# Retention followed by a gated feed-forward layer: the second layer's 512-column products issued as two 256-column products

## The chip, the cores and the metric

The kernel runs on one core of one Trainium2 chip. The metric is device time in microseconds (us), as the median of several runs; lower is better. The profile is one further execution, taken by the hardware profiler.

## What is computed

The first half is a retention layer: for every batch and head a 64 x 64 state decays by a factor gamma and takes up the outer product of k and v at every token; the output is q times the state. The second half is a feed-forward layer with a short convolution as its gate. Cut to what matters:

```python
# B, H, S, D = 4, 8, 768, 64; d_model 512, d_ff 1024
state = gamma * state + k[t] outer v[t]
y[t] = scale * q[t] @ state
x = y as (B, S, 512)
h = relu(x @ w_in)                       # first layer, 512 -> 1024
gate = sigmoid(conv3(h, conv_w))         # over neighbouring tokens
out = (h * gate) @ w_out                 # second layer, 1024 -> 512
```

## The kernel before

The tokens are worked through in 24 steps of 64 tokens of two batches; three steps make a unit of 384 rows, and there are 8 units. TensorE (PE) does three kinds of work: the retention's small products (64 x 64, `multiply`, line 592), the first layer (`mm1`, line 743: 12 products for each of 8 blocks of hidden channels and each unit, with 382 to 386 moving columns) and the second layer (`mm2`, lines 818 to 825). To keep accuracy, each operand is split into a head and a rest in fp32r, and a product of two such operands is three products: head by head, head by rest, rest by head.

`mm2(u, t, p, h)` takes tile t (128 rows) of unit u and the pair p of hidden blocks: two blocks of 128 channels, three products each. The stationary operand is 128 x 128 values of g (gated hidden values); the moving operand is w[:, cs], a slice of the second layer's weights. `columns` (line 814) gives the slice: all 512 columns, except for the very last tile, which is done as two halves of 256 columns (h = 0, 1). The sum over the 4 pairs is gathered in one PSUM bank (2 KB a partition, 512 fp32 columns) of the four called ps_yo; `put` (line 833, ScalarE) then copies it to SBUF, and a DMA writes it out. The first layer's sums lie in two banks called ps_m, which `relu` (line 760, ScalarE) empties.

Every matmul in fp32 or fp32r brings its own weight load: in the trace each MATMUL has its LDWEIGHTS, which the profile lists as a row of its own engine name, PEld.

The order of each engine's work is written out by hand, letter by letter, in the table `ORDER` (lines 65 to 88); `o` in PE's string is one call of `mm2`. The function `plan` (line 273) goes through these strings with a cost for each task, and sets only in which order the engines' tasks are recorded against each other and which buffer each one takes. `list_tasks` (line 141) holds the costs; line 262 is that of `mm2`.

Of the kernel before, what the change touches and what calls it, by code (L numbers as in the profile page):

```python
# [20 lines left out]
DM, DFF = H * D, 1024  # L21
# [3 lines left out]
NF = DFF // P  # L25
# [107 lines left out]
def act(n, fixed=85):  # L133
    return fixed + n / 1.2, 110 + fixed + n / 1.2


def matmul(n):
    return max(113, 4.7 + 0.4427 * n)


def list_tasks():
# [3 lines left out]
    def task(key, engine, ns, after=(), take=(), free=(), count=0):  # L145
        after = [a if isinstance(a[0], tuple) else (a, 0) for a in after or () if a]
        tasks[key] = (engine, *ns, after, list(take), list(free), count)

    def load(key, n_bytes, after=(), take=()):
        task(key, DMA, (DMA_ISSUE, n_bytes), after, take)  # L150

    def pe(key, ns, after=(), take=(), free=(), count=0):
        task(key, PE, (ns, ns + 165), after, take, free, count)
# [10 lines left out]
    for n in range(N_STEPS):  # L164
        c, u = n % NC, UNIT_OF[n]
        first, width = FIRST_STEP[u], UNITS[u]
# [7 lines left out]
        if wide:  # L174
            pe(("scores", n), 1250, [("load_q", n), ("load_k", n)], banks, count=16)
            for j in range(2):
                last = [("g", "t")] if (n, j) == (WIDE - 1, 1) else []
# [29 lines left out]
    for i in [*range(NF), CONV, *range(NF, CONV)]:  # L207
        n = NF * 3 if i == CONV else 512
# [10 lines left out]
    for u, width in enumerate(UNITS):  # L219
        n0, n1 = FIRST_STEP[u], FIRST_STEP[u] + width  # L220
        body, cols = G * width * C, G * (TOKENS[u][1] - TOKENS[u][0])
        x = [("x_rest", n) for n in range(n0, n1 + (TOKENS[u][1] % C > 0))]
        for f in range(NF):
            p, odd = divmod(f, 2)
            h, cv, g = ("hc", ("h", u, p)), ("hc", ("cv", u, p)), ("g", (u, p))
            before = [("w_rest", f), f and ("mm1", u, f - 1)]
            take = [("ps_m", (u, f))]
            n = cols
            if u == 0 and f < SPLIT:
                n = G * P  # L230
                after = [("w_rest", f), f and ("mm1_wide", f - 1), ("x_rest", 0), ("x_rest", 1)]
                pe(("mm1_wide", f), 12 * matmul(n), after, take, count=12)
                before, take, n = before + [("mm1_wide", f)], [], cols - n
# [20 lines left out]
    for u, width in enumerate(UNITS):  # L254
        for p in range(NP):
            tiles = sorted(range(width), key=lambda t: u == LAST[0] and t != 1)
            for t, h in [(t, h) for t in tiles for h in range(1 + ((u, t) == LAST))]:
                cols = DM // (1 + ((u, t) == LAST))
                o, ps, g = ("t2", ("o", u, t, h)), ("ps_yo", ("o", u, t, h)), ("g", (u, p))
                need = [("g_rest", u, p), p and ("mm2", u, t, p - 1, h), ("w_rest", NF + 2 * p), ("w_rest", NF + 2 * p + 1)]  # L260
                ends = t == width - 1 and cols * (h + 1) == DM
                pe(("mm2", u, t, p, h), 6 * matmul(cols), need, [] if p else [ps], [g] * ends, 6)
                if p == NP - 1:
                    task(("put", u, t, h), ACT, act(cols, 45), [("mm2", u, t, p, h)], [o], [ps])
                    if u == LAST[0]:
                        load(("out", u, t, h), 4 * P * cols, [("put", u, t, h)])
                    else:
                        pieces = 1 + (t * P // (width * C) < ((t + 1) * P - 1) // (width * C))
                        task(("out", u, t, h), POOL, (550 * pieces, 550 * pieces + 1850), [("put", u, t, h)])
# [84 lines left out]
def retention_then_gated_ffn(  # L354
# [12 lines left out]
    nc = tc.nc  # L367
# [36 lines left out]
    ps_st = psum.tile([P, G, NPAIR, D], F32, name="ps_st")  # L404

    tasks = list_tasks()
    emitted, slot, more = plan(tasks)

    tiles = {}

    def buf(name, owner):

        if (name, owner) not in tiles:
            label = f"{name}_{slot[name, owner]}"
            if name in sizes:
                made = pool.tile([P, sizes[name]], F32R if name in ("xu", "g") else F32, name=label, bufs=1)
            else:
                made = psum.tile([P, 512], F32, name=label, bufs=1)
            tiles[name, owner] = made
        return tiles[name, owner]  # L420
# [23 lines left out]
    def g_of(u, p):  # L444
        t = UNITS[u] * C
        return buf("g", (u, p))[:, : 4 * G * t].rearrange("p (i f b t) -> p i f b t", i=2, f=2, b=G)
# [270 lines left out]
    def w_parts(i):  # L717
        return [split[i][:, k] for k in range(2)]
# [95 lines left out]
    def columns(u, t, h):  # L814
        return slice(h * DM // 2, (h + 1) * DM // 2) if (u, t) == LAST else slice(0, DM)

    @emits
    def mm2(u, t, p, h):
        cs = columns(u, t, h)
        ps = buf("ps_yo", ("o", u, t, h))[:, : cs.stop - cs.start]  # L820
        for f in (2 * p, 2 * p + 1):
            hi, lo = (g_of(u, p)[:, i, f % 2].rearrange("p b t -> p (b t)")[:, t * P : (t + 1) * P] for i in range(2))
            w_hi, w_lo = w_parts(NF + f)
            for i, (g, w) in enumerate(((hi, w_hi), (hi, w_lo), (lo, w_hi))):
                nc.tensor.matmul(ps, g, w[:, cs], start=(f == 0 and i == 0), stop=(f == NF - 1 and i == 2))  # L825

    def put_tiles(u, t, h):
        cs = columns(u, t, h)
# [23 lines left out]
    for i in range(WARM_SMALL):  # L852
        j, cross, at = i % 2, i // 2 % 2, i // 4 * D
        ps = banks[cross + 2 * (at // 512)]
# [81 lines left out]
```

## Time and profile before

| what | value |
|---|---|
| median of 3 runs | 340.3 us |
| lowest and highest run | 340.2 and 342.24 us |
| profiled execution, span from first to last instruction | 537.5 us |
| mean granted TensorE clock in the profiled execution | 0.560 |
| PE busy | 533.2 us, 99% of the span |
| weight loads (PEld) busy | 380.3 us, 71% |
| VectorE (DVE) busy, ScalarE (ACT) busy | 206.4 us, 188.6 us |

The profiled execution is 1.58 times as long as the median run: the power throttle granted the array 0.56 of its clock throughout it after the first 6.7 us. No separate device time is listed for the profiled execution; its span is what the views divide up. PE's busy time is the union of its matmuls from start to modelled end; since matmuls are pipelined, the mean duration of one matmul is longer than its distance to the next.

### The profile page before, as it was taken

Reading aid. Unit: us, or ns where it says so; the run is one execution under the profiler, and the core shown is the slowest. Engines: PE = TensorE matmul, PEld = TensorE weight load, DVE = VectorE, ACT = ScalarE, POOL = GpSimd, SP = SyncE. Lnnn points to the kernel's source line nnn. Section 1 sums busy time; section 2 is a strip of 40 time slices with the busy share of each in tenths; the row PEclk is TensorE's granted clock in tenths of the full one; section 3 lists DMA queues with packets and bytes.
Section 4 is the critical chain, followed back from the end, with each engine's and each line's share of the span. In section 5 each row is a group of like instructions: output and inputs, shape, how many; then the busy total and the mean of one; then the engine's idle time right before and its main releaser. Section 6 shows DMA issues by size and latency. Waiting matters only on the chain.

```text
span 537.5 us, 9902 instructions
## 1 busy us (share of the span) xinstructions
PE 533.2 (99%) x4315; PEld 380.3 (71%) x4315; DVE 206.4 (38%) x323; ACT 188.6 (35%) x367; POOL 36.9 (7%) x96
## 2 busy tenths in 40 slices
PE   9999999999999999999999999999999999999997
PEld 6988887777667577767767676776676676666575
DVE  2644247747555332603345021524133213333300
ACT  3757356353425423302425120442134023422301
POOL 1000000110002000010002000100001000200100
PEclk7555555555555555555555555555555555555555
DMA  8763693401225032113024000100001000100101
GB/s 291 233 238 129 191 330 97 141 4 38 79 71 205 0 79 79 61 39 99 21 79 146 32 1 0 40 21 1 0 1 40 20 1 20 34 6 1 48 11 59
DMA packets 20935, 40.15 MB, mean 75 GB/s; under 512 B 2854, under 2 KB 3116, under 8 KB 20892
## 3 DMA queue, kind: packets, MB, share of 16 engines
q1 hardware_dynamic: 19100, 34.01, 19.2%
q0 software_dynamic: 1792, 5.51, 3.3%
q8 instruction: 34, 0.56, 0.4%
q14 instruction: 9, 0.07, 0.0%
HBM read 33.21 MB, written 6.29 MB: 73 GB/s over the span
## 4 chain that ended last, share of the span: by engine, by line
PE 99%; ACT 0%; issue 0%; DVE 0%
PE ps_m L743 42%; PE ps_yo L825 41%; PE ps_s L592 6%; PE ps_st L592 5%; PE ps_yo L592 4%; PE ps_yo L458 1%; PE ps_yo L555 0%; PE ps_m L458 0%; ACT t L833 0%; PE ps_m L592 0%; DVE warm L449 0%
## 5 line engine op out<-in xcount | busy, mean ns | idle before, releaser
L743 PE MATMUL ps_m<-xu,w 128*128 128x384 f32 (+4 forms) x780 | 230.9, 476 | 0.0
L825 PE MATMUL ps_yo<-w,g 128*128 128x512 f32 (+1 forms) x600 | 228.8, 561 | 0.0
L743 PEld LDWEIGHTS ps_m<-xu,w 128*128 128x128 f32 x780 | 169.7, 223 | 55.0 <-issue 5.6
L825 PEld LDWEIGHTS ps_yo<-w,g 128*128 128x128 f32 x600 | 129.7, 223 | 82.3 <-issue 45.1
L793 DVE SCALAR_TENSOR_TENSOR hc<-hc,cw_sb,hc 128x384 f32<-128x384 f32 (+1 forms) x128 | 75.3, 613 | 96.2 <-ACT hc L788 88.6
L760 ACT ACTIVATE hc<-ps_m 128x384 f32<-128x384 f32 (+2 forms) x64 | 31.2, 490 | 187.8 <-PE ps_m L743 182.8
L592 PE MATMUL ps_yo<-rw 64*64 64x64 f32 (+1 forms) x1408 | 73.1, 283 | 0.0
L592 PEld LDWEIGHTS ps_yo<-rw 64*64 64x64 f32 (+1 forms) x1408 | 68.7, 198 | 1.5 <-issue 1.1
L812 DVE TENSOR_TENSOR g<-hc,g 128x768 fp32r<-128x768 f32 x32 | 30.5, 954 | 50.6 <-ACT g L807 50.5
L592 PEld LDWEIGHTS ps_s<-rw 64*64 64x64 f32 (+1 forms) x720 | 36.9, 194 | 11.4 <-issue 8.9
L807 ACT CAST g<-hc 128x768 fp32r<-128x768 f32 x32 | 26.5, 831 | 44.2 <-PE ps_yo L825 43.3
L592 PE MATMUL ps_s<-rw 64*64 64x64 f32 (+1 forms) x720 | 41.1, 281 | 0.0
L803 DVE TENSOR_TENSOR hc<-hc,hc 128x768 f32<-128x768 f32 x32 | 30.2, 952 | 27.3 <-ACT hc L798 27.3
L788 ACT ACTIVATE hc<-hc,cw_sb 128x384 f32<-128x384 f32 x64 | 38.2, 614 | 1.3 <-POOL hc L778 1.2
L592 PE MATMUL ps_st<-rw 64*64 64x64 f32 (+1 forms) x672 | 36.4, 285 | 0.0
L643 DVE TENSOR_TENSOR rw<-ps_s,mask 128x512 f32<-128x512 f32 x22 | 15.1, 687 | 53.7 <-PE ps_s L592 46.5
L592 PEld LDWEIGHTS ps_st<-rw 64*64 64x64 f32 (+1 forms) x672 | 35.0, 204 | 0.2
L672 DVE TENSOR_TENSOR xu<-ps_yo,xu 128x512 fp32r<-128x512 f32 (+2 forms) x29 | 16.9, 595 | 46.9 <-ACT xu L667 46.9
L833 ACT COPY t<-ps_yo 128x512 f32<-128x512 f32 (+1 forms) x25 | 14.1, 565 | 50.4 <-PE ps_yo L825 49.9
L798 ACT ACTIVATE hc<-hc 128x768 f32<-128x768 f32 x32 | 26.8, 840 | 3.7 <-DVE hc L793 3.7
L845 POOL DMA_DIRECT2D out_y<-t x28 | 15.5, 557 | 168.2 <-ACT t L833 123.3
L667 ACT CAST xu<-ps_yo 128x512 fp32r<-128x512 f32 (+2 forms) x29 | 14.4, 516 | 22.3 <-PE ps_yo L592 22.3
(46 smaller groups left out, 154.7 us busy)
## 6 DMA issues: line engine op xcount, KB each, us to landing
rw<-in_qk SPq DMA_DIRECT2D x48, 256.0 KB, 3.5
rw<-in_kv SPq DMA_DIRECT2D x46, 256.0 KB, 4.4
w<-in_w_in SPq DMA_DIRECT2D x16, 256.0 KB, 5.3
w<-in_w_out SPq DMA_DIRECT2D x16, 256.0 KB, 5.4
out_y<-t POOLq DMA_DIRECT2D x14, 256.0 KB, 2.3
out_y<-t POOLq DMA_DIRECT2D x14, 128.0 KB, 2.5
out_y<-t SPq DMA_DIRECT2D x4, 128.0 KB, 2.0
out_y<-t SPq DMA_DIRECT2D x1, 256.0 KB
```

The costliest lines, as they stand in the source:

```text
L592: nc.tensor.matmul(out, lhsT, rhs, start=start, stop=stop, skip_group_check=True)
L672: nc.vector.tensor_tensor(out=lo, in0=y, in1=hi.bitcast(F32), op=ALU.subtract)
L743: nc.tensor.matmul(ps, w[:, k], x[:, k], start=first and i == 0, stop=(i == len(products) - 1), skip_group_check=True)
L760: nc.scalar.activation(h, buf("ps_m", (u, f))[:, : G * t].rearrange("p (b t) -> p b t", b=G), AF.Relu)
L788: nc.scalar.activation(cv, h, AF.Copy, scale=w)
L793: nc.vector.scalar_tensor_tensor(out=cv, in0=h, scalar=w, in1=cv, op0=ALU.mult, op1=ALU.add)
L798: nc.scalar.activation(cv, cv, AF.Sigmoid)
L803: nc.vector.tensor_tensor(out=cv, in0=h, in1=cv, op=ALU.mult)
L807: nc.scalar.copy(g_of(u, p)[:, 0], cv_of(u, 2 * p))
L812: nc.vector.tensor_tensor(out=lo, in0=cv_of(u, 2 * p), in1=hi.bitcast(F32), op=ALU.subtract)
L825: nc.tensor.matmul(ps, g, w[:, cs], start=(f == 0 and i == 0), stop=(f == NF - 1 and i == 2))
L845: (nc.sync if u == LAST[0] else nc.gpsimd).dma_start(out[r0 : r0 + n, columns(u, t, h)], o[at - t * P : at - t * P + n])
```

## The change

Each product of `mm2` is issued as products of 256 columns: the first for columns 0 to 255 and the second for 256 to 511 of the slice, both with the same stationary operand and into the two halves of the same bank. The tile that already had 256 columns keeps its single product. Only the very first product into a bank carries the start flag. The cost that `plan` uses for `mm2` is written in the same units; the strings of `ORDER` are the same.

```diff
-                pe(("mm2", u, t, p, h), 6 * matmul(cols), need, [] if p else [ps], [g] * ends, 6)
+                n = 6 * cols // (DM // 2)
+                pe(("mm2", u, t, p, h), n * matmul(DM // 2), need, [] if p else [ps], [g] * ends, n)
...
             for i, (g, w) in enumerate(((hi, w_hi), (hi, w_lo), (lo, w_hi))):
-                nc.tensor.matmul(ps, g, w[:, cs], start=(f == 0 and i == 0), stop=(f == NF - 1 and i == 2))
+                for at in range(cs.start, cs.stop, DM // 2):
+                    o = ps[:, at - cs.start : at - cs.start + DM // 2]
+                    first, last = f == 0 and i == 0 and at == cs.start, f == NF - 1 and i == 2
+                    nc.tensor.matmul(o, g, w[:, at : at + DM // 2], start=first, stop=last, skip_group_check=True)
```

PE's program at the first calls of `mm2`, before the change (ps_yo and ps_m are the PSUM banks, w the weights, g the gated values, xu the first layer's input; x3 and x12 are equal instructions in a row):

```order
L825 MATMUL ps_yo_1339<-w_1109,g_1080 128x512 x3
L825 MATMUL ps_yo_1339<-w_1235,g_1080 128x512 x3
L743 MATMUL ps_m_1358<-xu_565,w_981 128x386 x12
L825 MATMUL ps_yo_1384<-w_1109,g_1080 128x512 x3
L825 MATMUL ps_yo_1384<-w_1235,g_1080 128x512 x3
L743 MATMUL ps_m_1396<-xu_890,w_377 128x384 x12
```

The same place of PE's program with the change:

```order
L829 MATMUL ps_yo_1339<-w_1109,g_1080 128x256 x6
L829 MATMUL ps_yo_1339<-w_1235,g_1080 128x256 x6
L744 MATMUL ps_m_1364<-xu_565,w_981 128x386 x12
L829 MATMUL ps_yo_1390<-w_1109,g_1080 128x256 x6
L829 MATMUL ps_yo_1390<-w_1235,g_1080 128x256 x6
L744 MATMUL ps_m_1408<-xu_890,w_377 128x384 x12
```

Three products of 512 columns have become six of 256; nothing has changed places with anything. This holds for all 184 such rows of PE's program, and the rows of the other engines stand in the same sequence in both.

PE's program in the last unit, before the change, where the last tile (ps_yo_4115 and ps_yo_4122) is done in halves:

```order
L825 MATMUL ps_yo_4093<-w_1109,g_4013 128x512 x3
L825 MATMUL ps_yo_4093<-w_1235,g_4013 128x512 x3
L825 MATMUL ps_yo_4104<-w_1109,g_4013 128x512 x3
L825 MATMUL ps_yo_4104<-w_1235,g_4013 128x512 x3
L825 MATMUL ps_yo_4115<-w_1109,g_4013 128x256 x3
L825 MATMUL ps_yo_4115<-w_1235,g_4013 128x256 x3
L825 MATMUL ps_yo_4122<-w_1109,g_4013 128x256 x3
L825 MATMUL ps_yo_4122<-w_1235,g_4013 128x256 x3
```

The same place with the change:

```order
L829 MATMUL ps_yo_4597<-w_1109,g_4481 128x256 x6
L829 MATMUL ps_yo_4597<-w_1235,g_4481 128x256 x6
L829 MATMUL ps_yo_4614<-w_1109,g_4481 128x256 x6
L829 MATMUL ps_yo_4614<-w_1235,g_4481 128x256 x6
L829 MATMUL ps_yo_4631<-w_1109,g_4481 128x256 x3
L829 MATMUL ps_yo_4631<-w_1235,g_4481 128x256 x3
L829 MATMUL ps_yo_4638<-w_1109,g_4481 128x256 x3
L829 MATMUL ps_yo_4638<-w_1235,g_4481 128x256 x3
```

The last tile's rows are unchanged; the other two tiles' rows have doubled their count.

## Rows read from the trace of the kernel before

**Rows 1.** The page, busy time of each engine, and the slices of PE and its clock

```profile
PE 533.2 (99%) x4315; PEld 380.3 (71%) x4315; DVE 206.4 (38%) x323; ACT 188.6 (35%) x367; POOL 36.9 (7%) x96
...
PE   9999999999999999999999999999999999999997
...
PEclk7555555555555555555555555555555555555555
```

**Rows 2.** The page, the chain that ended last, by line

```profile
PE ps_m L743 42%; PE ps_yo L825 41%; PE ps_s L592 6%; PE ps_st L592 5%; PE ps_yo L592 4%; PE ps_yo L458 1%; PE ps_yo L555 0%; PE ps_m L458 0%; ACT t L833 0%; PE ps_m L592 0%; DVE warm L449 0%
```

**Rows 3.** Groups by line and shape: count | busy us, mean ns | idle before

```profile
L825 PE MATMUL ps_yo<-w,g 128*128 128x512 f32 x552 | 220.3, 577 | 0.0
L743 PEld LDWEIGHTS ps_m<-xu,w 128*128 128x128 f32 x780 | 169.7, 223 | 55.0 <-issue 5.6 <-ACT rw L651 0.2
L825 PEld LDWEIGHTS ps_yo<-w,g 128*128 128x128 f32 x600 | 129.7, 223 | 82.3 <-issue 45.1 <-DVE hc L793 0.2 <-DVE t L712 0.2
L743 PE MATMUL ps_m<-xu,w 128*128 128x384 f32 x372 | 111.1, 478 | 0.0
L743 PE MATMUL ps_m<-xu,w 128*128 128x382 f32 x192 | 58.2, 481 | 0.0
L743 PE MATMUL ps_m<-xu,w 128*128 128x386 f32 x192 | 57.9, 483 | 0.0
...
L825 PE MATMUL ps_yo<-w,g 128*128 128x256 f32 x48 | 9.9, 379 | 0.0
...
L743 PE MATMUL ps_m<-xu,w 128*128 128x256 f32 x12 | 2.5, 376 | 0.0
L743 PE MATMUL ps_m<-xu,w 128*128 128x128 f32 x12 | 2.3, 350 | 0.0
```

**Rows 4.** Windows: start, body and end of the span; busy us (count), clock, DMA

```profile
0.00:6.60 6.60, 5.39 (x107) 4.31 (x107) 0.17 (x1) 1.49 (x2) 2.40 (x12) 1.00 0.72 212
6.80:13.00 6.20, 6.20 (x46) 4.37 (x45) 3.31 (x6) 3.03 (x9) 0.00 (x0) 0.56 1.01 369
13.00:534.20 521.20, 521.20 (x4166) 371.61 (x4165) 202.94 (x317) 183.74 (x355) 34.51 (x84) 0.56 0.21 69
534.20:537.50 3.30, 0.20 (x2) 0.00 (x0) 0.00 (x0) 0.37 (x1) 0.00 (x0) 0.53 0.27 97
```

**Rows 5.** The chain in order of time: start us, length us, what

```profile
23.21 4.47 PE ps_m L743 x24
...
410.13 16.20 PE ps_yo L825 x42
...
495.22 39.20 PE ps_yo L825 x126
```

**Rows 6.** Windows: a stretch of 512-column, then one of 256-column products (PE, PEld first)

```profile
410.13:426.34 16.21, 16.21 (x45) 8.74 (x45) 8.23 (x12) 5.62 (x9) 1.14 (x3) 0.56 0.09 29
...
525.10:527.20 2.10, 2.10 (x13) 2.10 (x12) 0.00 (x0) 0.00 (x0) 0.00 (x0) 0.56 0.00 0
```

**Rows 7.** Line 825: weight loads, ns min/median/max

```profile
L825 PEld LDWEIGHTS ps_yo<-w,g x600: 186/188/362, 98.9 to 533.8; 128*128 128x128 f32 x150
```

**Rows 8.** Windows: the stages where ACT (fourth) and DVE (third) are busiest

```profile
40.00:100.00 60.00, 60.00 (x831) 48.50 (x826) 29.33 (x49) 31.59 (x67) 3.12 (x14) 0.56 0.50 168
100.00:200.00 100.00, 100.00 (x837) 70.41 (x836) 53.08 (x84) 41.74 (x82) 10.52 (x20) 0.56 0.26 83
```

**Rows 9.** Waits: who waited for whom, us in total, times, longest

```profile
ACT t L833 <- PE ps_yo L825: 49.9, 13, 15.4
...
PE ps_yo L458 <- DVE warm L449: 1.1, 1, 1.1
```

**Rows 10.** DMA queues: the instructions' own queue; packets, MB, share

```profile
q8 instruction: 34, 0.56, 0.4%
```

## The prediction

> **What bounds the kernel now.** I read the page's busy times first: PE is busy in 99% of the span, and in every one of the 40 slices but the last [rows 1]. The chain that ended last says the same in another way: nearly all of it is PE, 42% in the first layer and 41% in the second, the one that is changed [rows 2]. Then the waits: the only wait of PE in the list is 1.1 us at the very start, for the memset of the warm-up operand [rows 9]. So in the profiled execution a product costs what PE takes for it, and nothing hides it.
>
> One reservation runs through everything below. The profiled execution spans 537.5 us and the median run takes 340.3 us, a ratio of 0.633. In the profile the granted clock is 0.56 from 6.8 us on [rows 4], between the two levels of 1.2 and 2.4 GHz: 1.34 GHz on the mean. The timed runs cannot have had this: the large matmuls stream 552 x 512 + 48 x 256 + 372 x 384 + 192 x 382 + 192 x 386 + 12 x 256 + 12 x 128 = 589,824 columns [rows 3], which at 1.344 columns a ns are 438.9 us, more than the whole run. So the rows tell the mechanism at 0.56 of the clock, and I have to carry it over to a clock that I do not see. The sum is made against the span of the profiled execution and then taken to 340.3 us by the ratio, or by the bounds given.
>
> **The change: what it adds.** Nothing is removed in work: the columns streamed are the same. 552 products become 1,104, so 552 matmuls and 552 weight loads are added, since every fp32 matmul of the trace has its own load (600 and 600 at line 825) [rows 3]. The printed program shows them in place, six for three, with no other move. The question is what a boundary between two matmuls costs, and whether the added load is hidden.
>
> *The boundary, by two readings.* The chain has 42 products of 512 columns in a row in 16.20 us, 385.7 ns each [rows 5]. Its last stretch is 126 products in 39.20 us, of which 48 have 256 columns and 78 have 512: 39.20 - 78 x 0.3857 = 9.12 us, or 190.0 ns for one of 256 columns [rows 5]. Two of these are 380.0 ns, 5.7 ns less than one of 512; 552 times that is -3.1 us of the 537.5, or -2.0 us by the ratio. The groups say otherwise: 220.3 us / 552 = 399.1 ns and 9.9 / 48 = 206.3 ns, so a pair is 13.4 ns more, 7.4 us of 537.5 and 4.7 us by the ratio [rows 3]. The group's busy time also holds the modelled run-out of the last product of each burst, and the 256-column products come in only a few short bursts, so this end is too high; the chain's end rests on a difference and may be too low. Between them the trace is compatible with no cost at all at a clock of 0.56.
>
> *The boundary at the timed clock.* A fixed cost can hide behind a throttled clock and show at a faster one. Take the span apart: 13.0 us of start, 521.2 us of body, 3.3 us of end [rows 4]. If the body ran at the full clock it would take 521.2 x 0.56 = 291.9 us, together 308.2 us. The median is 32.1 us above that. If all of it were a fixed cost of the body's 4,166 matmuls, that would be 7.7 ns each; if the granted clock was simply 521.2 x 0.56 / (340.3 - 16.3) = 0.90, it would be 0 ns. I take the middle, 3.9 ns, since neither end is shown: 552 x 3.9 = 2.1 us, with 0 and 4.3 us as ends. (The Trainium skill, "TensorE: Matmul & The Clock Gate", section "Wait — 56ns, not 53.3ns?", states a fixed cost of about 2.5 ns for each matmul that shows only at the full clock. By that, as an estimate, the term would be 552 x 2.5 = 1.4 us; the trace shows this cost neither way, since its body is at 0.56.)
>
> *The load.* In the 512-column stretch the load unit is busy 8.74 of 16.21 us; in the 256-column stretch it is busy 2.10 of 2.10 us [rows 6]. The loads of line 825 have 82.3 us of idle time ahead of them now [rows 3], and this room is what the 552 new loads are put into. A load takes 186 ns at least and 188 at the median [rows 7], against 190.0 ns of a 256-column product. Two tight rows support that it still fits: the 24 products at 23.21 us, half of them 256 and half 128 columns, take 4.47 us [rows 5], so the twelve of 128 take (4.47 - 12 x 0.190) / 12 = 183 ns, where 128 columns would by themselves take 95 ns. That is the load's own pace: 183 ns, below 190 by 4%. So I cost the added loads at nothing, but the cover is nearly used up; if it fails, the price is that of the first rival. If loads kept their 183 ns at the timed clock, where the product takes 190.0 x 0.633 = 120.3 ns, the added cost would be 1,104 x 63 = 70 us; if they shrink with the clock, nothing. I take nothing, because the rows have both at one clock and the load below.
>
> (The skill's same page, Part 3, section "The mechanism", has a rule that speaks against this change: a weight load runs beside matmuls in flight only where the row groups differ, and here all loads use all rows. By it each added load would stand alone: 552 x 188 ns x 0.633 = 66 us. The trace speaks against it: load and matmul are both busy for all of the 2.10 us [rows 6].)
>
> *What is moved and what follows.* Nothing is reordered on any engine or queue. Each `mm2` of six products ends about 23 ns later, a stretch of 42 products 164 ns. The put behind it on ACT starts later, and with it the relu that is queued behind the put and frees a ps_m bank for PE. ACT now waits for line 825 with 49.9 us in total [rows 9], so it is early by much at 0.56; at the timed clock ACT's 31.59 us in the stage from 40 to 100 us stand against 60 x 0.633 = 38 us, and DVE's 53.08 us in the next stage against 63 us [rows 8], so the slack is thinner. There are 23 puts of such tiles; at 164 ns each the most this could cost is 3.8 us, the least is nothing or below (PE slower gives the others slack). I take 0.5 us. More instructions mean more fetches of code: 34 packets and 0.4% of the DMA time now [rows 10]; an eighth more, and in a stretch where each instruction lasts longest. Nothing for that. The last tile's four bursts are unchanged, so the end of 3.3 us stays.
>
> Sum: 2.1 + 0 + 0.5 = 2.6 us on 340.3, so 342.9 us, 0.8% more. At the profile's clock the same steps give 537.5 us plus or minus a few.
>
> **The rivals.**
>
> 1. *The load becomes the bound (slower).* Place: every `mm2`. For it: the load unit at 100% in the 256-column stretch [rows 6], 4% of margin. Against it: the margin is there, and the 48 products of 256 columns that already exist show no loss in the chain. It decides as soon as the load's pace at the timed clock is over the product's 120.3 ns. The median load by the ratio is 188 x 0.633 = 119.0 ns; if the fixed 7.7 ns worked out above falls to the load's handing over rather than to the streaming, it is 126.7, so 6.4 ns for each of 1,104 products: 7.1 us. With the 0.5 us: 347.9 us.
>
> 2. *No cost.* The boundary is hidden at the timed clock as it is at 0.56, or PE has small waits at the faster clock that take it up. For it: the chain's 190.0 against 385.7 ns [rows 5], and ACT and DVE at over 80% in the early stages at the timed clock [rows 8], which makes such waits likely. 340.3 to 341.0, say 340.6 us. Here also belongs that the change would not do what it says, the second load being left out because the operand is the same: the cost would vanish too. The rows of 600 loads for 600 matmuls speak against that [rows 3].
>
> 3. *Each added load stands alone*, as worked out above: 340.3 + 66 = 406 us. Rows 6 speak against it.
>
> **How the numbers follow.** About 1% is what a measurement of this kernel can tell from no change. The forecast has a chance of 0.51, with its own range from 341.2 to 345.5 (0 to 4.3 us for the boundary, a part of the 3.8 us for the waits); about a third of it, 0.16, lies above 343.7, the limit of 1%. The load rival has 0.25, all of it over the limit. No cost has 0.22, of which 0.02 for a gain over 1%, which would need more than the chain's -2.0 us. The third has 0.02. So faster 0.02, within 1% 0.35 + 0.20 = 0.55, slower 0.16 + 0.25 + 0.02 = 0.43. The range from 340.4 to 348.5 us leaves out a small part of the no-cost case, the upper third of the load rival and the third rival, under 0.2 in all.
>
> **What would show it.** In the profile of the changed kernel, line 829 must show 1,152 matmuls of 256 columns and as many loads. If the boundary costs what I say, the chain's stretches at line 829 have a distance within a few ns of half of what a 512-column product would take at the clock granted there, and PE's list of waits stays as short as it is. If the load binds, that distance is that of the load and does not follow the granted clock. If the put is what matters, PE has new waits ahead of line 744 for relu on ACT. The prediction is wrong if the time is over 345.5 us, or if the added time is mostly in PE's waits.

## The result, and the profile after

The changed kernel takes 342.97 us (median of 6 runs, 342.5 to 343.64) against 340.36 us before (6 runs, 339.84 to 342.24): a ratio of 1.007 with a 95% interval from 1.0049 to 1.009, or 1.7 to 3.1 us more. Run a second time, beside other kernels on one chip, it came to 1.0052 (1.0038 to 1.0065).

The profile after is from an execution at a granted clock of 1.00, where the profile shown of before had 0.56. Its numbers can therefore not be set beside [rows 1 to 8] one by one; the kernel before was profiled again (experiment 0) and had 1.00 too. Page of the changed kernel: busy times, slices, the chain by line, the groups of the second layer.

```profile
PE 333.6 (98%) x4867; PEld 325.0 (95%) x4867; DVE 204.4 (60%) x323; ACT 186.9 (55%) x367; POOL 48.1 (14%) x96
...
PE   8799999999999999999999999999999999999996
PEld 6689999999999999999999999999999999999995
...
PEclk9999999999999999999999999999999999999999
...
q8 instruction: 38, 0.62, 0.8%
...
PE ps_m L744 40%; PE ps_yo L829 40%; PE ps_s L593 5%; PE ps_st L593 4%; PE ps_yo L593 3%; DMA rw<-in_qk 3%; SPq L466 1%; DVE rw L543 0%; DVE w L730 0%; ACT t L837 0%; DVEq L543 0%
...
L829 PE MATMUL ps_yo<-w,g 128*128 128x256 f32 x1152 | 143.0, 281 | 0.0
L829 PEld LDWEIGHTS ps_yo<-w,g 128*128 128x128 f32 x1152 | 140.4, 188 | 0.5
```

The change did what it says: 1,152 products of 256 columns and as many loads, 552 more of each than in [rows 3]. The loads' idle time at this line is 0.5 us. Four more packets of instructions were fetched than in [rows 10].

PE's waits of over 1 us in the changed kernel (longest first in the view):

```profile
PE ps_s L593 <- DVE t L713: 1.3, 1, 1.3
PE ps_yo L593 <- DMA rw<-in_kv: 1.3, 1, 1.3
PE ps_yo L459 <- DVE warm L450: 1.1, 1, 1.1
```

None of them stands in the second layer: they are of the start, which has waits at this clock that [rows 9] did not have. Now the windows, cut at the first and the last product of the second layer. First the kernel before at 1.00 (experiment 0), then the changed kernel; columns are PE, PEld, DVE, ACT and POOL busy, then clock and DMA.

```profile
0.00:68.38 68.38, 64.73 (x1463) 59.45 (x1464) 46.49 (x78) 51.93 (x117) 9.29 (x27) 1.00 0.85 297
68.38:335.53 267.15, 267.15 (x2857) 237.98 (x2852) 158.06 (x246) 134.20 (x249) 38.53 (x69) 1.00 0.23 72
335.53:339.20 3.67, 0.28 (x3) 0.08 (x1) 0.00 (x0) 0.37 (x1) 0.00 (x0) 1.00 0.57 180
```

```profile
0.00:68.82 68.82, 64.28 (x1463) 59.24 (x1463) 46.54 (x78) 52.21 (x117) 9.84 (x27) 1.00 0.86 295
68.82:337.88 269.06, 269.06 (x3411) 265.67 (x3404) 157.90 (x246) 134.33 (x249) 38.27 (x69) 1.00 0.23 72
337.88:341.50 3.62, 0.28 (x3) 0.08 (x1) 0.00 (x0) 0.37 (x1) 0.00 (x0) 1.00 0.57 181
```

This is the reading that carries the rest. In the middle part PE is busy for all of it in both kernels, and the part is 269.06 - 267.15 = 1.91 us longer. The start, which holds none of the changed code, differs by 0.4 us, and it differs as much between executions of one kernel (below). The end is the same within 0.05 us.

PE's busy time counts each product to its modelled end, so a short wait could hide in it. The same middle part by line of the kernel shows where the time went. The kernel before: second layer, first layer, retention (PE, PEld, clock, DMA).

```profile
68.38:335.53 267.15, 140.77 (x599) 108.43 (x600) 1.00 0.23 72
68.38:335.53 267.15, 110.16 (x588) 103.49 (x588) 1.00 0.23 72
68.38:335.53 267.15, 28.47 (x1670) 26.48 (x1664) 1.00 0.23 72
```

The changed kernel, in the same sequence:

```profile
68.82:337.88 269.06, 142.68 (x1152) 140.35 (x1152) 1.00 0.23 72
68.82:337.88 269.06, 110.16 (x588) 101.40 (x588) 1.00 0.23 72
68.82:337.88 269.06, 28.47 (x1671) 26.48 (x1664) 1.00 0.23 72
```

Rows of different lines overlap at their modelled ends, so the three add up to more than the part. The second layer has 142.68 - 140.77 = 1.91 us more of PE's time, and the other two lines have not moved by 0.01 us. Nor is there a new wait behind the second layer's stretches: from their last 512 columns to the next work PE takes 253 ns on the mean of the starts before and 258 ns after, some 4 ns more, as for any other pair. So the added time stands in the second layer's own products.

### The profile page after: what moved, and what is told of

Same layout as the page of the kernel before. It is cut to its first block, busy times and chain, and to the rows that moved or that the text cites. A ratio compares the mean times of both kernels' runs of the same rounds, so it can differ in the third digit from the quotient of the medians.

```text
span 341.5 us, 11005 instructions
## 1 busy us (share of the span) xinstructions
PE 333.6 (98%) x4867; PEld 325.0 (95%) x4867; DVE 204.4 (60%) x323; ACT 186.9 (55%) x367; POOL 48.1 (14%) x96
## 4 chain that ended last, share of the span: by engine, by line
PE 93%; DMA 3%; SPq 1%; DVE 0%; issue 0%; ACT 0%; DVEq 0%
PE ps_m L744 40%; PE ps_yo L829 40%; PE ps_s L593 5%; PE ps_st L593 4%; PE ps_yo L593 3%; DMA rw<-in_qk 3%; SPq L466 1%; DVE rw L543 0%; DVE w L730 0%; ACT t L837 0%; DVEq L543 0%
## 5 line engine op out<-in xcount | busy, mean ns | idle before, releaser
L744 PE MATMUL ps_m<-xu,w 128*128 128x384 f32 (+4 forms) x780 | 144.5, 338 | 0.2 <-DVE w L730 0.2
L829 PE MATMUL ps_yo<-w,g 128*128 128x256 f32 x1152 | 143.0, 281 | 0.0
L744 PEld LDWEIGHTS ps_m<-xu,w 128*128 128x128 f32 x780 | 133.6, 188 | 1.4 <-DVE w L730 0.4
L593 PE MATMUL ps_yo<-rw 64*64 64x64 f32 (+1 forms) x1408 | 47.5, 221 | 1.7 <-DMA rw<-in_kv 1.3
L593 PEld LDWEIGHTS ps_yo<-rw 64*64 64x64 f32 (+1 forms) x1408 | 43.8, 135 | 2.3 <-DMA rw<-in_kv 1.6
L593 PEld LDWEIGHTS ps_s<-rw 64*64 64x64 f32 (+1 forms) x720 | 24.5, 136 | 5.6 <-DVE t L713 1.7
L593 PE MATMUL ps_s<-rw 64*64 64x64 f32 (+1 forms) x720 | 27.7, 223 | 1.3 <-DVE t L713 1.3
L779 POOL COPY hc<-edge_sb 128x8 f32<-128x8 f32 (+1 forms) x24 | 14.1, 599 | 70.5 <-DVE hc L804 55.8
L775 POOL COPY edge_sb<-hc 128x8 f32<-128x8 f32 (+1 forms) x24 | 13.6, 573 | 73.1 <-ACT hc L761 73.1
L593 PE MATMUL ps_st<-rw 64*64 64x64 f32 (+1 forms) x672 | 23.7, 219 | 0.0
L644 DVE TENSOR_TENSOR rw<-ps_s,mask 128x512 f32<-128x512 f32 x22 | 15.1, 685 | 14.2 <-PE ps_s L593 13.4
```

The costliest lines, as they stand in the source:

```text
L593: nc.tensor.matmul(out, lhsT, rhs, start=start, stop=stop, skip_group_check=True)
L744: nc.tensor.matmul(ps, w[:, k], x[:, k], start=first and i == 0, stop=(i == len(products) - 1), skip_group_check=True)
L829: nc.tensor.matmul(o, g, w[:, at : at + DM // 2], start=first, stop=last, skip_group_check=True)
```

## Experiments

Theories: the **boundary** (a fixed cost for each added matmul, load hidden), the **load** (a weight load sets the distance of the 256-column products), the **waits** (later puts delay PE elsewhere).

**Experiment 0: the kernel before, profiled again.** No edit.

> The kernel before, unchanged, to have its trace at a granted clock of 1.00 (the first profile had 0.56). In the changed kernel at 1.00 the 256-column products follow each other at about 118.5 ns. Boundary theory (a fixed cost for each matmul, load hidden): one of 512 columns at 231 to 233 ns, so a pair costs 4 to 6 ns more, and PE's waits are as in the changed kernel. Waits theory (the later puts delay PE): 512 columns at 237 ns, and some 2.6 us less of waits of PE than in the changed kernel.

The span is 339.2 us at a clock of 1.00. The same two stretches of line 825 in the chain as in [rows 5], 42 products in a row and the last 126, kernel before:

```profile
260.28 9.75 PE ps_yo L825 x42
...
312.04 23.78 PE ps_yo L825 x126
```

The same stretches of the changed kernel:

```profile
261.92 9.91 PE ps_yo L829 x84
...
314.08 24.09 PE ps_yo L829 x204
```

A product of 512 columns takes 9.75 / 42 = 232.1 ns, one of 256 takes 9.91 / 84 = 118.0 ns. A pair is 236.0 ns, 3.9 ns more than one; the last stretch says 0.31 us / 78 = 4.0 ns. Boundary theory holds; PE's waits differ only at the start (1.3 us of waiting for a transfer of k or v in the changed kernel, 0.2 us here). The waits theory falls: it needed 237 ns here. That wait in this trace:

```profile
PE ps_yo L592 <- DMA rw<-in_kv: 0.2, 1, 0.2
```

From the two distances a line: (232.1 - 118.0) / 256 = 0.446 ns a column and 3.9 ns fixed for each product. The first layer's products are a check that did not go into it: the line gives 175 ns for 384 columns, and the median distance of two such products in this trace is 174 ns. Whether the 3.9 ns belong to the matmul or to the change to its new weights cannot be told, since every product has a load of its own.

**Experiment 1: 320 and 192 columns.**

```diff
-                for at in range(cs.start, cs.stop, DM // 2):
+                at = cs.start
+                for n in (320, 192) if cs.stop - cs.start == DM else (DM // 2,):
...
+                    at += n
```

> Each 512-column product as 320 and 192 columns: as many matmuls and loads as in the changed kernel, same columns. Boundary theory with a load pace of about 112 ns (the 128-column products of the changed kernel's trace stand 112 ns apart): 320 columns take about 146 ns and the 192 are held at the load's 112, so a pair takes 258 instead of 237 ns: 552 x 21 = 12 us over the changed kernel, 355 us. If loads cost nothing at all and only the count of matmuls matters: 343.0 us, as the changed kernel. Load theory (118 ns of the 256-column product is the load's own pace): a pair of 264 ns, 358 us.

Measured: 354.91 us, ratio 1.0413 (1.0394 to 1.0433). The last stretch of its chain:

```profile
324.30 25.87 PE ps_yo L830 x204
```

48 of these 204 are the unchanged 256-column products, 48 x 0.118 = 5.66 us; the other 78 pairs take 20.21 / 78 = 259.1 ns. By the line of experiment 0 a product of 320 takes 146.5 ns by its columns, which leaves 112.6 ns for one of 192, where its columns need 89.5. The starts of the load rows in this stretch show the same without the line: they stand 111 and 145 ns apart by turns, 111 while a product of 192 columns runs. So the same count of matmuls and the same columns cost 12 us more than the changed kernel: the count alone is not the price, the load has a pace of its own, and that pace is below 118 ns. This is what the boundary theory expected (258 ns a pair); the load theory needed 264 ns and falls.

**Experiment 2: 384 and 128 columns.** The same edit with (384, 128).

> Each 512-column product as 384 and 128 columns. Boundary theory with a load pace of 112 ns: 175 + 112 = 287 ns a pair, 552 x 50 = 28 us over the changed kernel, 371 us. Count of matmuls alone: 343.0 us. Load theory with a pace of 118 ns: 293 ns a pair, 374 us. The distance of the 128-column products in the trace gives the pace itself.

Measured: 369.71 us, ratio 1.0853 (1.0823 to 1.0884). The last stretch:

```profile
336.15 28.05 PE ps_yo L830 x204
```

(28.05 - 5.66) / 78 = 287.0 ns a pair; 384 columns take 175.0 by the line, so 112.0 ns are left for the second. The two uneven splits give one pace, and the load rows again stand 111 ns apart while the short product runs.

**Experiment 3: half-outer order.**

```diff
-            for i, (g, w) in enumerate(((hi, w_hi), (hi, w_lo), (lo, w_hi))):
-                for at in range(cs.start, cs.stop, DM // 2):
+            products = ((hi, w_hi), (hi, w_lo), (lo, w_hi))
+            for at in range(cs.start, cs.stop, DM // 2):
+                for i, (g, w) in enumerate(products):
```

> The same 256-column products, but the three of one half first and then the three of the other, so that no two products in a row have the same stationary operand (but where the head of g follows itself within a half). Boundary and load theories: as the changed kernel, 343.0 us within 0.5. If a repeated stationary operand is loaded more cheaply in the changed kernel: slower here by up to 552 x 5 ns = 2.8 us, 345.8 us.

Measured: 342.13 us, but beside a kernel before of 341.06 us on that chip: ratio 1.0043 (1.0029 to 1.0057), which overlaps with the 1.007 of the changed kernel and left it open whether this order is a little better. The next two runs settle it.

**Experiments 4 and 5: the changed kernel and the half-outer order again, on one chip.**

> The changed kernel again, beside the half-outer order on the same chip. In the traces at 1.00 the time from the first to the last product of the second layer is 267.15 us before, 269.05 us here and 269.05 us in the half-outer order, while the time up to the first of these products spreads from 67.2 to 68.8 us over five traces. If that is all: 1.9 us over the kernel before, a ratio of 1.0055, equal to the half-outer order within 0.5 us. If the order of the halves matters: 1.0 to 1.5 us slower than the half-outer order again.

> The half-outer order again on the same chip as the changed kernel: the same time within 0.5 us, ratio 1.0055 to the kernel before, first to last product 269.05 us. If the order of the halves matters: 1.0 to 1.5 us faster than the changed kernel.

Measured: 342.3 us, ratio 1.0052 (1.0038 to 1.0065), and 342.75 us, ratio 1.0066 (1.0053 to 1.0078): no difference that could be told, and this time with the other sign. The windows from the first to the last product of the second layer, changed kernel of experiment 4:

```profile
68.49:337.55 269.06, 269.06 (x3410) 265.68 (x3404) 157.89 (x246) 134.25 (x249) 38.21 (x69) 1.00 0.22 72
```

Half-outer order of experiment 3:

```profile
67.22:336.27 269.05, 269.05 (x3409) 265.67 (x3404) 157.94 (x246) 134.31 (x249) 38.33 (x69) 1.00 0.23 72
```

All four traces with the split in every unit have 269.05 or 269.06 us here, whichever the order. What moves from run to run is where the part begins: 67.22, 68.37, 68.49 and 68.82 us. So the order of the halves does not matter to the time. That a repeated stationary operand is not loaded more cheaply does not follow from this: the half-outer order still repeats two of six, and the loads lie hidden under the products in both orders. Experiment 7, where the load sets the pace, shows it.

**Experiment 6: 288 and 224 columns.** The edit of experiment 1 with (288, 224).

> Each 512-column product as 288 and 224 columns. By the first two uneven splits a load takes 109 to 111 ns and runs beside the product ahead of it. A product of 224 columns is then 118.5 - 32 x 0.45 = 104 ns, so 5 to 7 ns of the load stay uncovered: 552 x 6 = 3.3 us over the changed kernel, 272.4 us from the first to the last product, 346 us. If the load were covered down to 192 columns and the loss came suddenly there: as the changed kernel.

Measured: 347.4 us, ratio 1.0209 (1.0193 to 1.0224), and 273.76 us for the part, where 272.4 was expected. The part and its last stretch:

```profile
67.96:341.72 273.76, 273.76 (x3408) 270.39 (x3404) 157.93 (x246) 134.22 (x249) 36.88 (x69) 1.00 0.22 70
```

```profile
317.27 24.74 PE ps_yo L830 x204
```

(24.74 - 5.66) / 78 = 244.6 ns a pair; 132.3 by the line for 288 columns leaves 112.3 ns. I had put the load at 109 to 111 ns; at 112 the loss comes out. The cover does not break suddenly: with 224, 192 and 128 columns in the short product the loss grows with the columns that are missing.

**Experiment 7: four times 128 columns.** The edit with (128, 128, 128, 128).

> Each 512-column product as four of 128: 1,656 matmuls and loads more than before, all held at the load's pace. Boundary theory with a load pace of 110 ns: 440 ns for each product of before instead of 234, so 552 x 0.206 = 114 us over the kernel before, 454 us. If loads and matmuls overlapped without limit: 4 x (0.45 x 128 + 3) = 243 ns, 346 us.

Measured: 459.14 us, ratio 1.3484 (1.3459 to 1.3509), 5 us over what was expected from a pace of 110 ns.

```profile
413.54 40.53 PE ps_yo L830 x360
```

(40.53 - 5.66) / 312 = 111.8 ns for each product of 128 columns: here nothing but the load sets the distance. Four measurements of it agree, 111.8 to 112.6 ns. In this kernel ten of twelve products in a row have the stationary operand of the one before, and their loads last to the next one as long as those of a new operand (111 to 113 ns, by place in the twelve). A repeated operand is loaded again in full.

**Experiment 8: the kernel before, a further trace.** No edit.

> The kernel before once more, for a second trace at a granted clock of 1.00: if the part from the first to the last product of the second layer is as steady as in the four traces with 256-column products (269.05 us each), it is 267.15 us again, within 0.05 us.

```profile
68.53:335.69 267.16, 267.16 (x2859) 237.96 (x2852) 158.05 (x246) 134.22 (x249) 38.42 (x69) 1.00 0.23 72
```

267.16 us: the part is as steady in the kernel before, and the difference of 1.9 us is therefore one of the programs and not of the executions.

**Experiment 9: the split in units 0 to 3 alone.**

```diff
+            step = DM // 2 if u < 4 else cs.stop - cs.start
...
-                for at in range(cs.start, cs.stop, DM // 2):
+                for at in range(cs.start, cs.stop, step):
```

> The split in units 0 to 3 alone: 288 of the 552 products. Boundary theory: 3.44 ns for each added matmul wherever it stands, so the part from the first to the last product takes 267.15 + 0.99 = 268.14 us, and the whole 1.0 us more than before, ratio 1.003. If the loss comes from a few places where other engines are late (the first units, where ACT and DVE are busiest): all 1.9 us here, 269.05 us; if from the last units: 267.15 us.

Measured: 341.34 us, ratio 1.0025 (1.0005 to 1.0045). The part from the first to the last product and, from the chain, the last stretch:

```profile
67.65:335.73 268.08, 268.08 (x3146) 252.71 (x3140) 157.96 (x246) 134.31 (x249) 38.22 (x69) 1.00 0.22 72
```

```profile
312.24 23.78 PE ps_yo L830 x126
```

268.08 us, 0.93 us over the kernel before: 3.2 ns for each of 288 added matmuls. The last stretch, in a unit that is not split, takes the 23.78 us of the kernel before. The loss stands where the splits are, in proportion to their number: 0.93 of 1.91 us for 288 of 552 splits.

## Why the prediction was right, and where its working was not

342.9 us was predicted, 342.97 measured. That the two agree within 0.1 us is luck: the sum held 0.5 us of waits that did not come, and the traces show 1.9 us for what the measured medians put at 2.6. The mechanism was right: a small fixed cost for each added product, with the load hidden. Step by step:

- *PE bounds it, and a product costs what PE takes.* Right. Between the first and the last product of the second layer PE is busy in all of the time, at this clock too.
- *The boundary: 3.9 ns, 2.1 us.* Right in size: 3.9 ns in long stretches, 1.91 us / 552 = 3.5 ns over the whole part (by the starts of their products, the two longest stretches have 3.9 and 4.0 ns, the many short ones 3.3 on the mean; why was not tried). But the working that led to it was half luck. It gave the 32.1 us between the scaled span and the median either to a clock below full (0.90) or to a fixed cost for each matmul (7.7 ns), and took the middle. The runs show a third reading for about half of it: the clock granted is 1.00, and a column takes 0.446 ns instead of the 0.417 that 2.4 GHz would give. On 589,824 columns that is 17 us, which is neither of my two ends; the other half was not taken apart. The working also left the 13.0 us of the start at the clock of the profile, and its range begins at 341.2 us, where an end of 0 for the boundary would give 340.3. The two bounds at 0.56 were poor: by the chain a pair was 5.7 ns cheaper [rows 5], by the groups 13.4 ns dearer [rows 3], and the sign of the first is wrong at 1.00. At 0.56 the distances did not show the fixed cost.
- *The load at nothing.* Right, by experiments 1, 2, 6 and 7: its pace is 112 ns, 6 ns below the product's 118.0. The margin is 5%, near the 4% read from [rows 5] at the other clock: the load's pace shrank from 183 to 112 ns and the product's distance from 190.0 to 118.0.
- *Rival 1, the load as the bound, 126.7 ns.* It did not come, and its price was mis-sized: I scaled the load's duration of 188 ns [rows 7] by the ratio of the times. Its row has the same 186 and 188 ns at 1.00:

```profile
L829 PEld LDWEIGHTS ps_yo<-w,g x1152: 186/188/193, 68.8 to 337.8; 128*128 128x128 f32 x192
```

  That duration is not what the load holds the unit for: in experiment 7 one follows the other every 112 ns. The mechanism of this rival is real, though. By the line it decides below 256 - 6 / 0.446 = some 243 columns, which is an estimate between two measured lengths: 256 columns did not pay for it, and experiment 6, with 224, paid 5 us against the changed kernel of the same chip.
- *The waits, 0.5 us.* Wrong: nothing came. The list has no wait of PE in that part, in spite of ACT and DVE being busier beside a faster PE; the time of the first layer and of the retention did not move by 0.01 us, and experiment 9 shows the loss in proportion to the splits.
- *Rival 2, no cost:* fallen, by 267.15 and 267.16 against 269.05 to 269.06 us. A second load for the same operand is not left out (1,152 rows) and not cheaper (experiment 7).
- *Rival 3 and the rule on row groups:* fallen. With loads standing alone a pair would take its columns' time and two times 112 ns. It is the distance of 118 ns that shows this, and not that both rows are busy for all of 2.10 us [rows 6], since PE's busy time runs to modelled ends. The Trainium skill, "TensorE: Matmul & The Clock Gate", Part 3, section "The mechanism", lets a load run beside matmuls only where row groups differ. The trace does not agree: all loads of the second layer use all rows, and they run beside the product ahead, for 112 of its 118 ns. The opening of the same section also names a background weight buffer, for which a load is pulled ahead; that is in keeping with these rows, and nothing here shows the buffer itself.

The 2.61 us of the first comparison is 0.7 more than the 1.9 us of the traces; the second comparison gave 0.52% of 340.5, 1.8 us. The difference is within the intervals, and the start part, which spreads by 1.6 us over executions, is enough for it.

## What to carry to other kernels

Splitting a product costs little as long as each part takes longer than the weight load that runs beside it: then only a small fixed cost is paid for each added product, here 4 ns. Below that length (an estimate of 243 columns of fp32r here; 256 were long enough, 224 were not) every missing column is paid in full, and an uneven split pays for its smaller part. Look at the length of the shortest product before the count of products. Read the pace of a load from the distance of products that are known to be shorter than it, not from the duration in its row.

## What the runs showed that was not expected

At a granted clock of 1.00 a column of these fp32r products takes 0.446 ns, as if the array ran at 2.24 GHz, and this follows from the difference of 512 and 256 columns, so that no fixed cost can be in it. What takes the 7% was not tried. The first trace speaks against a full clock of 2.24 GHz: at 0.56 of that a column would take 0.80 ns, and the trace has 385.7 / 512 = 0.75 [rows 5], where 0.56 of 2.4 GHz gives 0.74. So most of the 7% shows at the full clock alone, and a distance read at 0.56 cannot be scaled by the clock: 385.7 x 0.56 = 216 ns, where 232.1 was measured. (The Trainium skill, "TensorE: Matmul & The Clock Gate", section "Wait — 56ns, not 53.3ns?", has N / 2.4 GHz and 2.5 ns for back-to-back matmuls. By that, as an estimate, a product of 512 columns would take 215.8 ns, where the trace has 232.1; the measurement decides here.)

The profile shown of before had 0.56 from 6.8 us to its end, while every later profile had 1.00 for the same kernel and one like it; the time of the runs had already excluded 0.56. What set it, the power limit or anything else, was not tried.
